# Attention and feed-forward in one kernel: the first two chunk passes taken in halves

## Chip, cores and metric

The kernel runs on one core of one Trainium2 chip. The metric is the device time of one execution in microseconds; several runs of a kernel are compared by their median. TensorE is called PE here, VectorE DVE, ScalarE ACT, GpSimd POOL and SyncE SP, as the profile calls them.

## The reference

Block-sparse attention (4 batches, 8 heads, 768 positions of 64, blocks of 32; each block sees its neighbours, the first and last block and three sampled ones; the first and last block see all) feeds a feed-forward layer of 512 to 2048 to 512 over all 3072 tokens:

```python
attn = softmax(where(mask, q @ k.T / sqrt(64), -1e9)) @ v
x = attn.transpose(0, 2, 1, 3).reshape(3072, 512)
h = x @ w_in
out = (h - tanh(h)) @ w_out
```

## The kernel before

The weights `w_in` and `w_out` come as 64-bit words. Each is cut into 16 tiles `ft` of 128 columns or rows (512 KB as words). A tile is loaded (`load`), turned into 32-bit floats by three DVE instructions (`convert`, which need a scratch of one PSUM bank), and split into a high and a low part by one ACT and one POOL instruction (`split`), so that a product is made of three matmuls. Tiles with `ft < KEPT` (3) stay in SBUF; the others go to scratch in HBM and are read again for every later chunk. Before the change, chunk 0 writes the unsplit 256 KB tile out (`w1`), chunk 1 reads it back, splits it a second time (`again`, `split`) and writes the split 512 KB tile (`w2`), and from chunk 2 on the split tile is read (`get`).

The tokens are cut into six chunks of 512 columns (`CHUNKS`: four blocks of 32 for all batches). A feed-forward unit `u` is one chunk with one `ft`: 12 matmuls make `h` in bank 4 or 5 (`first`), ACT, DVE and POOL make `h - tanh(h)` (`bent`), and two and a half units later 12 matmuls add its product with `w_out` to four banks 0 to 3 (`second`). After the 16 units of a chunk the four banks are copied out and stored (`store`).

An attention unit is one block and half of the heads: `scores` (PE), `most` (DVE maximum), `exps` (ACT), `turn` (PE transposes), `copy`, `accum` (PE), `norm` (DVE), `put` (ACT and POOL write the two parts of a column block of the chunk's operand `x`). There are 44 of these and 12 more for the edge blocks (`weigh`, `join`). Eight (units 0 to 7) must be done before chunk 0 can start, in the lead; units 8 and 9 start in the lead too. After the lead, attention has banks 6 and 7 to itself, except that `convert` of most weight tiles takes bank 6 as its scratch.

The order on every engine is the order of a plan: each step is entered by `at(time, ...)`, where the time is counted in feed-forward units, and all steps are issued sorted by that time. Engines take their instructions in that order, SP its DMAs too.

Of the kernel before, what the change touches and what calls it, by code (L numbers as in the profile page):

```python
# [22 lines left out]
P = 128  # L23
# [7 lines left out]
CT = 4  # L31
# [50 lines left out]
@with_exitstack  # L82
def attention_ffn(ctx, tc, k, q, v, samp, w, rows, out):
    nc = tc.nc
    pool = lambda name, bufs=1, **kw: ctx.enter_context(tc.tile_pool(name=name, bufs=bufs, **kw))
    cst, dpool = pool("cst"), pool("dpool", space=DRAM)
    ident = cst.tile([P, P], F32, name="ident")
    make_identity(nc, ident)
    bias = [cst.tile([P, 1], F32, name=f"bias{i}") for i in range(2)]
    for x, val in zip(bias, (QB, THR2)):  # L90
        nc.vector.memset(x, val)
    banks = [t for psum in [pool("psum", space=PSUM)] for t in [psum.tile([P, 512], F32, name=f"ps{i}") for i in range(8)]]
    f2, rv = pool("f2", 2), pool("rv", 2)
    plan = []

    def at(time, f, *args):
        plan.append((time, len(plan), f, args))

    ffn = FFN(tc, w, bias, banks, dpool, f2, pool("xb"), pool("wb", 3), pool("wr"), rv, out)
    Attention(tc, k, q, v, samp, rows, ffn, ident, banks, pool("att"), pool("sm", 4), f2, rv, at)  # L100
    ffn.plan(at)
    for _, _, f, args in sorted(plan, key=lambda e: e[:2]):
        f(*args)


class Unit:
# [3 lines left out]
    def __init__(self, n, c, time, b=None, f=None, k=None):  # L110
        self.n, self.c, self.b, self.f, self.k = n, c, b, f, k
        early = n < LEAD
        if early:
            t = lambda x: (n + x - T0) * RATE
            self.t = dict(s=t(0.3), m=t(0.65), e1=t(1.1), e0=t(1.2), turn=t(2.0), c0=t(2.15), c1=t(2.2), pv=t(2.6), norm=t(3.05))
        else:
            t = lambda x: time + x
            self.t = dict(s=t(0), m=t(0.08), e1=t(0.2), e0=t(0.3), turn=t(TURN), c0=t(TURN + 0.06), c1=t(TURN + 0.05), pv=t(PROD), norm=t(PROD + 0.1))
        self.banks = dict(s=((6, 7), (0, 1))[n % 2], t=(2, 3), o=4 + n % 2) if early else dict(s=(6, 7), t=(6, 7), o=7)
# [6 lines left out]
class Attention:  # L126
    def __init__(self, tc, k, q, v, samp, rows, ffn, ident, banks, att, sm, f2, rv, at):
# [29 lines left out]
        for m, blocks in enumerate(CHUNKS[1:]):  # L157
            steps = [(c, dict(b=b)) for b in blocks if 0 < b < NB - 1 for c in range(2)]
            if m:
                steps += [((m - 1) // 2, dict(f=(m - 1) % 2, k=k)) for k in range(3)]  # L160
            for i, (c, kw) in enumerate(steps):
                add(c, FIRST0 + SPACE0 * (i + 8 - LEAD) if m == 0 else NFT * m + FIRST + SPACE * i, **kw)
# [8 lines left out]
        for u in units:  # L171
            t, n = u.t, u.n
            if u.b:
                if n:
                    at(max(t["s"] - 2.0, units[n - NQ].t["s"] + 0.01) if n >= NQ else lead(-8.95 + 0.01 * n), self.load_q, u)
                at(max(t["s"] - 1.2, u.before.t["s"] + 0.01 if u.before else lead(-3)), self.gather_k, u)
                at(max(t["s"] - 2.0, u.before.t["pv"] + 0.01 if u.before else lead(-3)), self.gather_v, u)
            else:
                if u.k == 0:
                    at(units[n - 1].t["s"] + 0.02, self.load_q, u)  # L180
                at(units[n - 2].t["pv"] + 0.02, self.load_ve, u)
            at(t["s"], self.scores, u)
            at(t["m"], self.most, u)
            at(t["e1"], self.exps, u, 1)
            at(t["e0"], self.exps, u, 0)
            at(t["turn"], self.turn, u)
            at(t["c1"], self.copy, u, 1)
            at(t["c0"], self.copy, u, 0)
            at(t["pv"], self.accum, u)
            at(t["norm"], self.norm, u)  # L190
            if u.b:
                for x in "hl":
                    at(t["norm"] + (0.1 if x == "h" else 0.15), self.put, u, x)
            elif u.k == 2:
                at(t["e0"] + 0.12, self.weigh, u)
                end = u.n == len(units) - 1
# [219 lines left out]
    def join(self, u, k, s):  # L416
# [15 lines left out]
class FFN:  # L432
    def __init__(self, tc, words, bias, banks, dpool, f2, xb, wb, wr, rv, out):
        self.nc = InOrder(tc)
        self.words, self.bias, self.out = words, bias, out
        self.f2, self.xb, self.wb, self.rv = f2, xb, wb, rv
        self.banks, self.acc, self.hb = banks, banks[:4], banks[4:6]
        kept = [(m, ft) for m in "io" for ft in range(NFT)]
        self.one = {w: dpool.tile([P, 512], F32, name="w1{}{}".format(*w)) for w in kept if w[1] >= KEPT}
# [32 lines left out]
    def split(self, m, u):  # L472
        ft = u % NFT
        t = self.work.pop((m, ft))
        if ft >= KEPT:
            if u < NFT:
                self.nc.sync.dma_start(out=self.one[m, ft], in_=t.bitcast(F32))
        to = self.parts(m, u)
        hi, lo = self.w[m, u]
        self.nc.scalar.activation(out=hi, in_=t.bitcast(F32), func=AF.Copy)  # L480
        self.nc.gpsimd.tensor_tensor(out=lo, in0=t.bitcast(F32), in1=hi.bitcast(F32), op=ALU.subtract)
        if u >= NFT:
            self.nc.sync.dma_start(out=self.two[m, ft], in_=to.bitcast(F32))

    def again(self, m, u):
        t = self.work[m, u % NFT] = self.f2.tile([P, 512], F32, tag="wcvt", name=f"re{m}{u}")
        self.nc.sync.dma_start(out=t, in_=self.one[m, u % NFT])

    def get(self, m, u):
        self.nc.sync.dma_start(out=self.parts(m, u).bitcast(F32), in_=self.two[m, u % NFT])  # L490

    def operand(self, n):
        if n not in self.x:
            t = self.xb.tile([P, 2, NCT, 512], F32R, tag=f"x{n % 2}", name=f"x{n}")
# [3 lines left out]
    def first(self, u, c):  # L498
        xh, xl = self.x[u // NFT]
# [73 lines left out]
    def plan(self, at):  # L573
        conv = sorted(((m, ft) for ft in range(NFT) for m in "io"), key=lambda w: w[1] + NEED[w[0]])
# [5 lines left out]
        for k, ((m, ft), (t0, dt, tmp)) in enumerate(zip(conv, slots)):  # L580
            at(max(t0 - 1.8, done[k - 3] + 0.01 if k > 2 else -99), self.load, m, ft, k)
            for x in range(3):
                at(t0 + dt * x, self.convert, m, ft, x, tmp)
            done.append(t0 + 2 * dt)
            at(done[k] + 0.03, self.split, m, ft)
        for u in range(NU):
            for m, g in (("i", GETI), ("o", GETO)):
                if u % NFT < KEPT:
                    self.w[m, u] = tuple(self.res[m, u % NFT][:, x] for x in range(2))
                elif u >= 2 * NFT:  # L590
                    at(u + g, self.get, m, u)
# [58 lines left out]
```

## Time and profile before

| | |
|---|---|
| median of 3 runs | 803.07 us (802.23 to 804.96) |
| profiled execution, its own time | 805.06 us |
| its span, first to last instruction | 803.3 us |
| mean granted TensorE clock | 0.975 |
| PE busy | 745.8 us |
| DVE, ACT, POOL busy | 554.5, 485.0, 346.2 us |
| moved by DMA | 152.34 MB, mean 190 GB/s |

The profiled execution is 1.76 us longer than its span and 1.99 us above the median. A time in a row is counted from the start of the span. The clock column is the share of full speed granted to TensorE: 1.00 is 2.4 GHz and 0.50 is 1.2 GHz.

### The profile page before, as it was taken

Reading aid. Unit: us, or ns where it says so; the run is one execution under the profiler, and the core shown is the slowest. Engines: PE = TensorE matmul, PEld = TensorE weight load, DVE = VectorE, ACT = ScalarE, POOL = GpSimd, SP = SyncE. Lnnn points to the kernel's source line nnn. Section 1 sums busy time; section 2 is a strip of 40 time slices with the busy share of each in tenths; the row PEclk is TensorE's granted clock in tenths of the full one; section 3 lists DMA queues with packets and bytes.
Section 4 is the critical chain, followed back from the end, with each engine's and each line's share of the span. In section 5 each row is a group of like instructions: output and inputs, shape, how many; then the busy total and the mean of one; then the engine's idle time right before and its main releaser. Section 6 shows DMA issues by size and latency. Waiting matters only on the chain.

```text
span 803.3 us, 20749 instructions
## 1 busy us (share of the span) xinstructions
PE 745.8 (93%) x8128; PEld 571.4 (71%) x8128; DVE 554.5 (69%) x982; ACT 485.0 (60%) x1031; POOL 346.2 (43%) x410
## 2 busy tenths in 40 slices
PE   1777797988999999999999999999999999999996
PEld 0555575766777777777777777777777778888884
DVE  4575877888776676677776677766668667666654
ACT  1684756667587677666655655666567564554543
POOL 3683755768466655543422244322333132222211
PEclk9898898999999999999999999999999999999999
DMA  8978566667268677546665336574526555336542
GB/s 320 309 228 243 175 185 186 191 160 235 87 191 270 236 261 236 192 142 229 194 222 192 94 120 196 196 276 134 178 61 191 203 175 184 131 104 237 183 158 78
DMA packets 57077, 152.34 MB, mean 190 GB/s; under 512 B 9363, under 2 KB 16020, under 8 KB 56980
## 3 DMA queue, kind: packets, MB, share of 16 engines
q1 hardware_dynamic: 56596, 150.49, 58.6%
q8 instruction: 64, 1.05, 0.6%
q10 hardware_dynamic: 384, 0.52, 0.2%
q14 instruction: 33, 0.27, 0.1%
HBM read 124.24 MB, written 26.74 MB: 188 GB/s over the span
## 4 chain that ended last, share of the span: by engine, by line
PE 74%; DVE 1%; ACT 1%; POOL 1%; issue 1%; DMA 0%; POOLq 0%; DVEq 0%
PE ps L68 74%; DVE ps L68 1%; POOL wi L68 0%; ACT p L68 0%; DMA out<-ob 0%; POOL kr L68 0%; DVE cvto L68 0%; DVE x L68 0%; POOL t L68 0%; DVE cvti L68 0%; DVE rs L68 0%; ACT hs L68 0%; ACT pt L68 0%; ACT t L68 0%; POOL wo L68 0%
## 5 line engine op out<-in xcount | busy, mean ns | idle before, releaser
L68 PE MATMUL ps<-x,wi 128*128 128x512 f32 x936 | 239.8, 399 | 1.7 <-ACT wo L68 0.9
L68 POOL TENSOR_TENSOR gl<-t,gh 128x512 fp32r<-128x512 f32 x96 | 124.3, 1295 | 240.8 <-ACT gh L68 110.5
L68 PEld LDWEIGHTS ps<-x,wi 128*128 128x128 f32 x936 | 173.3, 189 | 46.5 <-issue 6.6
L68 PE MATMUL ps<-wo,gh 128*128 128x512 f32 x624 | 202.5, 407 | 0.0
L68 PEld LDWEIGHTS ps<-wo,gh 128*128 128x128 f32 x624 | 114.9, 191 | 33.1 <-issue 7.8
L68 PE MATMUL ps<-wo,gl 128*128 128x512 f32 x312 | 123.6, 398 | 0.3 <-POOL gl L68 0.3
L68 ACT ACTIVATE u<-ps 128x512 f32<-128x512 f32 x96 | 57.1, 595 | 87.8 <-PE ps L68 86.9
L68 POOL COPY kr<-ks 128x256 f32 (+2 forms) x182 | 94.9, 615 | 17.8 <-DMA ks<-k 14.2
L68 DVE TENSOR_TENSOR t<-t,ps 128x512 f32<-128x512 f32 x80 | 54.6, 683 | 64.2 <-ACT t L68 64.1
L68 DVE TENSOR_REDUCE m<-ps 128x2 f32<-128x512 f32 x112 | 72.0, 684 | 37.7 <-PE ps L68 33.0
L68 PE MATMUL ps<-kr,q 64*32 64x256 f32 x1408 | 57.1, 408 | 31.8 <-POOL kr L68 16.1
L68 POOL TENSOR_TENSOR x<-xt,x 128x256 fp32r<-128x256 f32 (+1 forms) x46 | 33.9, 737 | 104.4 <-ACT x L68 104.4
L68 DVE COPY_PREDICATED t<-mk,ps 128x512 f32<-128x512 int32 x96 | 71.4, 744 | 6.3
L68 ACT ACTIVATE p<-ps,nb 128x256 f32<-128x256 f32 x176 | 73.9, 471 | 2.9
L68 DVE SCALAR_TENSOR_TENSOR ps<-qq,ps 128x512 f32<-128x512 f32 x96 | 66.4, 692 | 10.8 <-ACT qq L68 4.9
L68 DVE TENSOR_TENSOR ps<-ps,u 128x512 f32<-128x512 f32 x96 | 66.4, 691 | 5.9 <-ACT t L68 5.9
L68 PEld LDWEIGHTS ps<-wo,gl 128*128 128x128 f32 x312 | 59.4, 190 | 15.2 <-POOL gl L68 1.0
L68 ACT ACTIVATE qq<-u,bias 128x512 f32<-128x512 f32 x96 | 69.5, 724 | 0.0
L68 ACT ACTIVATE mk<-u,bias 128x512 f32<-128x512 f32 x96 | 69.1, 720 | 0.0
L68 DVE SCALAR_TENSOR_TENSOR ps<-u,ps 128x512 f32<-128x512 f32 x96 | 66.3, 691 | 1.9
L68 PEld LDWEIGHTS ps<-vw,pt 128*32 128x32 f32 x2816 | 44.5, 113 | 30.2 <-ACT pt L68 11.3
L68 PE MATMUL ps<-ident,p 128*128 128x128 f32 x448 | 62.0, 283 | 3.5 <-DVE cvto L68 3.5
(86 smaller groups left out, 961.5 us busy)
## 6 DMA issues: line engine op xcount, KB each, us to landing
wi<-w2i SPq DMA_DIRECT2D x52, 512.0 KB, 4.4
wo<-w2o SPq DMA_DIRECT2D x52, 512.0 KB, 3.9
vw<-v SPq DMA_DIRECT2D x182, 130.0 KB, 3.3
q<-q SPq DMA_DIRECT2D x52, 128.0 KB, 4.3
w2i<-wi SPq DMA_DIRECT2D x13, 512.0 KB, 3.9
w2o<-wo SPq DMA_DIRECT2D x13, 512.0 KB, 3.8
ve<-v SPq DMA_DIRECT2D x24, 260.0 KB, 5.9
ks<-k SPq DMA_DIRECT2D x8, 768.0 KB, 6.6
```

The costliest lines, as they stand in the source:

```text
L68: r = f(*args, **kw)
```

## The change

Chunk 0 runs over the units 0 to 7 (called 0A here), then chunk 1 over 0 to 7 (1A) and 8 to 15 (1B), then chunk 0 over 8 to 15 (0B). After 0A the four banks are copied out and kept in HBM (`keep`), and added again when 0B is stored (`back`, `store`). A weight tile is split once, right after its conversion, and only the split tile is saved (`save`); for `ft` of 8 and more the split is written over the words it came from. Sixteen tiles are converted in the lead and 0A, the other sixteen between units 8.35 and 22.5, one every 0.94 units, on banks 6 and 7 by turns. The attention units of chunk 1 stand 1.14 units apart in 0A (2.3 before), none stands in 1A and most of 1B, and those of chunk 2 come 1.14 apart in 0B; these units are transposed 0.66 units after their scores (1.0 before). The edge steps come a chunk later. The lead is planned 0.95 steps earlier, units 8 and 9 get times and banks of their own, and four `q` tiles are held in place of three. POOL does the subtraction `t - h` for 32 units in place of 16.

```diff
-LEAD, T0, RATE = 10, 11.2, 0.62
-FIRST0, SPACE0, FIRST, SPACE, LATE, TURN, PROD = 0.2, 2.3, -1.5, 1.45, 71.0, 1.0, 1.33
-NQ = 3
+LEAD, T0, RATE = 10, 10.25, 0.62
+QUICK, TURN, PROD = (0.66, 0.95), 1.0, 1.33
+NQ = 4
-POOLED = range(NFT)
+POOLED = range(2 * NFT)
+SEGS = [(0, 0, HALF), (1, 0, HALF), (1, HALF, NFT), (0, HALF, NFT)] + [(n, 0, NFT) for n in range(2, len(CHUNKS))]
+BAND = [None, (0.75, 1.14), (22.72, 1.14), (31.87, 1.44), (47.71, 1.44), (63.55, 1.44)]
+EDGES = {3: (0,), 4: (1,), 5: (2, 3)}
+CONVA = [0.1, 0.75, 1.4, 2.05, 2.65, 3.31, 3.77, 4.45, 4.91, 6.05, 7.19, 7.62]
+CONVAB = [3, 3, 3, 3, 6, 7, 6, 7, 6, 6, 6, 6]
+CONVB = 8.35, 0.94
...
-    def split(self, m, u):
...
-            if u < NFT:
-                self.nc.sync.dma_start(out=self.one[m, ft], in_=t.bitcast(F32))
+        if ahead:
+            to = self.raw[m, ft].bitcast(F32R)
...
-    def again(self, m, u):
...
+    def save(self, m, ft):
+        self.nc.sync.dma_start(out=self.two[m, ft], in_=self.done[m, ft].bitcast(F32))
...
+    def keep(self, j):
...
+        self.nc.sync.dma_start(out=self.part[j], in_=t)
...
-        slots = [(t(3.3 + 1.6 * k), 0.3 * RATE, None) for k in range(3)] + [(0.1 + 0.4 * k, 0.1, banks[3]) for k in range(6)]
-        slots += [(FIRST0 + SPACE0 * k + x, 0.1, banks[6]) for k in range(1, 6) for x in (0.47, 1.2, 1.58, 1.95)]
-        slots += [(NFT + FIRST + x, 0.1, banks[6]) for x in (-0.47, 0.47, 1.2)]
+        slots = [(t(3.3 + 1.6 * k), 0.3 * RATE, None) for k in range(4)] + [(x, 0.09, banks[b]) for x, b in zip(CONVA, CONVAB)]
+        slots += [(CONVB[0] + CONVB[1] * k, 0.12, banks[6 + k % 2]) for k in range(2 * HALF)]
...
+            if ft >= KEPT:
+                at(end + 0.4, self.save, m, ft)
+            free.append(end + (1.2 if ahead else 0.01))
+            sent[m, ft] = end + 1.3
...
-                elif u >= NFT:
-                    at(u + g - 0.8, self.again, m, u)
-                    at(u + g + 0.3, self.split, m, u)
+                elif (m, u) not in done:
+                    at(max(u + g, sent[m, ft]), self.get, m, u)
```

On PE, at the end of the lead, the order before is this (`ps` 72 to 79 are banks 0 to 7; `kr,q` is `scores`, `ident,p` is `turn`, `vw,pt` is `accum`, `x,wri` is `first` of feed-forward unit 0). The first two rows are the `turn` of attention unit 8, then come its `accum` (its first and last row), the `turn` of unit 9, half of `first`, the `scores` of unit 10 (one row), the `accum` of unit 9 (one row) and the second half of `first`:

```order
L68 MATMUL ps_75<-ident,p_1_1074 128x128 x4
L68 MATMUL ps_74<-ident,p_0_1084 128x128 x4
L68 MATMUL ps_76<-vw_161,pt_1_1171 32x65 x4
...
L68 MATMUL ps_76<-vw_162,pt_0_1169 32x65 x4
L68 MATMUL ps_75<-ident,p_1_1166 128x128 x4
L68 MATMUL ps_74<-ident,p_0_1174 128x128 x4
L68 MATMUL ps_76<-x_455,wri_147 128x512 x6
L68 MATMUL ps_78<-kr_165,q_6_970 32x256
...
L68 MATMUL ps_77<-vw_163,pt_1_1232 32x65 x4
...
L68 MATMUL ps_76<-x_455,wri_147 128x512 x6
```

And this is the same place of the changed kernel:

```order
L79 MATMUL ps_75<-ident,p_1_1062 128x128 x4
L79 MATMUL ps_74<-ident,p_0_1070 128x128 x4
L79 MATMUL ps_76<-x_435,wri_128 128x512 x12
L79 MATMUL ps_73<-ident,p_1_1155 128x128 x4
L79 MATMUL ps_72<-ident,p_0_1163 128x128 x4
L79 MATMUL ps_79<-vw_139,pt_1_1160 32x65 x4
...
L79 MATMUL ps_79<-vw_140,pt_0_1158 32x65 x4
L79 MATMUL ps_78<-kr_143,q_6_954 32x256
```

All 12 matmuls of unit 0 now stand right behind the `turn` of attention unit 8; the `turn` of 9, the `accum` of 8 and 9 and the `scores` of 10 stand behind them.

On DVE, in the middle of 0A, the changed kernel has this order (`ps_79` and `ps_78` are banks 7 and 6; `m<-ps` is `most`, `rs`, `x`, `xt` is `norm`, rows with `raw` or `spare` are `convert`, `ps_76` and `ps_77` are `h`):

```order
L79 STREAM_TRANSPOSE xt_1741<-x_1745 128x256
L79 TENSOR_REDUCE m_1773<-ps_79 128x2
L79 TENSOR_REDUCE m_1773<-ps_78 128x2
L79 SCALAR_TENSOR_TENSOR ps_77<-qq_1687,ps_77 128x512
L79 TENSOR_SCALAR ps_79<-spare 128x512
L79 COPY_PREDICATED t_1660<-mk_1696,ps_77 128x512
L79 SCALAR_TENSOR_TENSOR ps_79<-spare,ps_79 128x512
L79 SCALAR_TENSOR_TENSOR cvto_1793<-spare,ps_79 128x512
L79 TENSOR_TENSOR ps_76<-ps_76,u_1803 128x512
L79 TENSOR_SCALAR ps_78<-rawi_1648 128x512
L79 SCALAR_TENSOR_TENSOR ps_78<-rawi_1648,ps_78 128x512
L79 SCALAR_TENSOR_TENSOR cvti_1843<-rawi_1648,ps_78 128x512
```

One conversion now stands between the maximum and the transposes of an attention unit (bank 7), the next one behind them (bank 6); before, four conversions on bank 6 stood between two attention units.

On SP, in 1B, the changed kernel has this order (`rawi`, `rawo` or `spare` from `w` is `load`, `w2` from one of these is `save`, `wi` or `wo` from `w2` is `get`; each moves 512 KB). What stood at the same row before is `accum`'s `vw` loads and the 256 KB `w1` tiles:

```order
L79 DMA rawi_2798<-w 128x1024
L79 DMA w2i_113<-spare 128x1024
L79 DMA wi_2808<-w2i_111 128x1024
L79 DMA wo_2845<-w2o_122 128x1024
L79 DMA spare<-w 128x1024
L79 DMA w2o_124<-rawo_2746 128x1024
L79 DMA wi_2863<-w2i_112 128x1024
L79 DMA wo_2900<-w2o_123 128x1024
```

For each unit there is now one load, one save and two gets, one behind the other.

## Rows read from the trace of the kernel before

**Rows 1.** Busy time by stretch: each engine's busy us (instructions), clock, DMA share, GB/s.

```profile
15.00:78.00 63.00, 47.97 (x1102) 33.93 (x1103) 38.92 (x83) 38.60 (x104) 39.16 (x62) 0.89 0.90 278
78.00:200.00 122.00, 102.84 (x930) 76.92 (x929) 98.77 (x169) 80.86 (x165) 86.04 (x89) 0.90 0.65 189
200.00:640.00 440.00, 438.76 (x5275) 334.98 (x5274) 310.37 (x556) 280.82 (x605) 179.90 (x218) 1.00 0.57 185
640.00:795.00 155.00, 155.00 (x823) 124.90 (x822) 100.34 (x154) 82.27 (x156) 38.65 (x35) 1.00 0.48 160
```

**Rows 2.** ACT in order of time: `qq` of units 0, 16, 32, 74 and 95.

```profile
78.15 0.74 ACT L68 ACTIVATE qq<-u,bias 128x512 f32<-128x512 f32 x1
...
214.15 0.72 ACT L68 ACTIVATE qq<-u,bias 128x512 f32<-128x512 f32 x1
...
342.14 0.74 ACT L68 ACTIVATE qq<-u,bias 128x512 f32<-128x512 f32 x1
...
672.52 0.72 ACT L68 ACTIVATE qq<-u,bias 128x512 f32<-128x512 f32 x1
...
789.14 0.72 ACT L68 ACTIVATE qq<-u,bias 128x512 f32<-128x512 f32 x1
```

**Rows 3.** Who waited for whom: us in total, times, longest us.

```profile
PE ps L68 <- DVE cvti L68: 7.8, 4, 2.9
...
PE ps L68 <- ACT pt L68: 6.7, 8, 3.1
...
PE ps L68 <- DVE cvto L68: 5.6, 3, 3.0
```

**Rows 4.** PE in order of time, two waits for conversions in chunk 0.

```profile
98.11 1.09 PE L68 MATMUL ps<-ident,p 128*128 128x128 f32 x4 [3.01 <-DVE cvto L68]
...
111.85 1.10 PE L68 MATMUL ps<-kr,q 64*32 64x256 f32 x32 [1.57 <-DVE cvti L68]
```

**Rows 5.** Two stretches, PE alone: busy, clock, DMA share, GB/s.

```profile
98.00:104.00 6.00, 5.89 (x53) 0.50 0.51 141
110.00:112.00 2.00, 0.43 (x10) 1.00 0.89 133
```

**Rows 6.** PE in order of time, end of the lead.

```profile
59.64 1.09 PE L68 MATMUL ps<-ident,p 128*128 128x128 f32 x8
63.48 0.45 PE L68 MATMUL ps<-vw,pt 128*32 128x65 f32 x8 [2.74 <-DMA vw<-v]
64.49 1.75 PE L68 MATMUL ps<-vw,pt 128*32 128x65 f32 x56 [0.57 <-DMA vw<-v]
...
70.31 1.09 PE L68 MATMUL ps<-kr,q 64*32 64x256 f32 x32
71.34 1.11 PE L68 MATMUL ps<-vw,pt 128*32 128x65 f32 x64
72.38 1.65 PE L68 MATMUL ps<-x,wri 128*128 128x512 f32 x6
```

**Rows 7.** POOL in order of time: the last `put` of attention unit 7.

```profile
63.20 0.73 POOL L68 TENSOR_TENSOR x<-xt,x 128x256 fp32r<-128x256 f32 x1 [1.31 <-ACT x L68]
```

**Rows 8.** PE in order of time: the wait of attention unit 3.

```profile
29.82 1.96 PE L68 MATMUL ps<-kr,q 64*32 64x256 f32 x32 [4.43 <-DMA q<-q]
```

**Rows 9.** Busy time by stretch, columns as in Rows 1.

```profile
10.00:30.00 20.00, 9.34 (x184) 5.58 (x192) 9.57 (x17) 8.32 (x23) 12.91 (x21) 0.97 1.03 363
110.00:120.00 10.00, 8.43 (x69) 6.40 (x68) 7.45 (x12) 6.54 (x16) 5.30 (x5) 1.00 0.89 229
...
280.00:300.00 20.00, 20.00 (x210) 15.71 (x213) 14.97 (x25) 15.32 (x34) 11.29 (x10) 1.00 0.80 266
700.00:800.00 100.00, 96.21 (x415) 77.52 (x413) 60.65 (x89) 49.61 (x88) 23.41 (x18) 1.00 0.46 149
```

**Rows 10.** DMA issues: count, KB each, median us from issue to landing.

```profile
wi<-w2i SPq DMA_DIRECT2D x52, 512.0 KB, 4.4
```

**Rows 11.** Groups of instructions: busy us, mean ns, idle before, releasers.

```profile
L68 ACT ACTIVATE ob<-ps 128x512 f32<-128x512 f32 x12 | 7.2, 601 | 4.4 <-PE ps L68 2.4 <-DMA out<-ob 2.0
```

More of the change, by code (lines that the diff above doesn't have):

```diff
@@ L97, in at @@
         plan.append((time, len(plan), f, args))
-    ffn = FFN(tc, w, bias, banks, dpool, f2, pool("xb"), pool("wb", 3), pool("wr"), rv, out)
-    Attention(tc, k, q, v, samp, rows, ffn, ident, banks, pool("att"), pool("sm", 4), f2, rv, at)
+    att = pool("att")
+    ffn = FFN(tc, w, bias, banks, dpool, f2, pool("xb"), pool("wb", 3), pool("wr"), rv, att, out)
+    Attention(tc, k, q, v, samp, rows, ffn, ident, banks, att, pool("sm", 4), f2, rv, at)
     ffn.plan(at)
@@ L106, with __init__ @@
 class Unit:
-    def __init__(self, n, c, time, b=None, f=None, k=None):
+    def __init__(self, n, c, time, b=None, f=None, k=None, quick=False):
         self.n, self.c, self.b, self.f, self.k = n, c, b, f, k
@@ L156, in __init__ @@
                 add(c, 0, b=b)
[L157 to L160, printed above, removed]
+        for m, blocks in list(enumerate(CHUNKS))[1:]:
+            steps = [(c, dict(b=b, quick=m < 3)) for b in blocks if 0 < b < NB - 1 for c in range(2)]
+            edges = [(g // 2, dict(f=g % 2, k=k)) for g in EDGES.get(m, ()) for k in range(3)]
+            steps += edges
             for i, (c, kw) in enumerate(steps):
-                add(c, FIRST0 + SPACE0 * (i + 8 - LEAD) if m == 0 else NFT * m + FIRST + SPACE * i, **kw)
+                add(c, BAND[m][0] + BAND[m][1] * (i - 2 * (m == 1)), **kw)
         lead = lambda x: (x - T0) * RATE
@@ L195, in __init__ @@
                 at(t["e0"] + 0.12, self.weigh, u)
-                end = u.n == len(units) - 1
+                end = 2 * u.c + u.f in EDGES[len(CHUNKS) - 1]
                 quiet = iter([t["norm"] + 0.1 + 0.08 * j for j in range(6)] if end else self.quiet(units[u.n + 1 :], t["norm"]))
@@ L432, with __init__ @@
 class FFN:
-    def __init__(self, tc, words, bias, banks, dpool, f2, xb, wb, wr, rv, out):
+    def __init__(self, tc, words, bias, banks, dpool, f2, xb, wb, wr, rv, att, out):
         self.nc = InOrder(tc)
         self.words, self.bias, self.out = words, bias, out
-        self.f2, self.xb, self.wb, self.rv = f2, xb, wb, rv
+        self.f2, self.xb, self.wb, self.rv, self.att = f2, xb, wb, rv, att
         self.banks, self.acc, self.hb = banks, banks[:4], banks[4:6]
         kept = [(m, ft) for m in "io" for ft in range(NFT)]
-        self.one = {w: dpool.tile([P, 512], F32, name="w1{}{}".format(*w)) for w in kept if w[1] >= KEPT}
+        self.part = [dpool.tile([P, 512], F32, name=f"part{j}") for j in range(CT)]
         self.two = {w: dpool.tile([P, 1024], F32, name="w2{}{}".format(*w)) for w in kept if w[1] >= KEPT}
@@ L442, in __init__ @@
         self.spare = xb.tile([P, 1024], I32, name="spare")
-        self.x, self.w, self.h, self.work, self.raw = {}, {}, {}, {}, {}
+        self.x, self.w, self.h, self.work, self.raw, self.done = {}, {}, {}, {}, {}, {}
     def parts(self, m, u):
-        if u % NFT < KEPT:
-            t = self.res[m, u % NFT]
+        ft = UNITS[u][1]
+        if ft < KEPT:
+            t = self.res[m, ft]
         else:
@@ L548, in second, with back @@
         g = [self.work[u, x] for x in ("gh", "gh", "gl")]
-        ft = u % NFT
+        first, last = u in (0, *self.ends), u + 1 in self.ends
         for i in part:
             self.nc.tensor.matmul(
-                self.acc[j], lhsT=g[i][:, j * P : (j + 1) * P], rhs=wo[i % 2], start=ft == i == 0, stop=ft == NFT - 1 and i == 2
+                self.acc[j], lhsT=g[i][:, j * P : (j + 1) * P], rhs=wo[i % 2], start=first and i == 0, stop=last and i == 2
             )
+    def keep(self, j):
+        t = self.att.tile([P, DM], F32, tag=("p0", "p1", "pt0", "pt1")[j], name=f"half{j}")
+        if j % 2:
+            self.nc.vector.tensor_scalar(out=t, in0=self.acc[j], scalar1=-1.0, scalar2=None, op0=ALU.mult)
+        else:
+            self.nc.scalar.activation(out=t, in_=self.acc[j], func=AF.Copy, scale=-1.0)
+        self.nc.sync.dma_start(out=self.part[j], in_=t)
+    def back(self, j):
+        if j % 2 == 0:
+            self.sums = self.rv.tile([P, 1040], F32, tag="rv", name=f"sums{j}")
+        self.work["sum", j] = self.sums[:, DM * (j % 2) : DM * (j % 2) + DM]
+        self.nc.sync.dma_start(out=self.work["sum", j], in_=self.part[j])
     def store(self, n, j):
@@ L580, in plan @@
-        for k, ((m, ft), (t0, dt, tmp)) in enumerate(zip(conv, slots)):
-            at(max(t0 - 1.8, done[k - 3] + 0.01 if k > 2 else -99), self.load, m, ft, k)
+        halves = [sorted(((m, ft) for ft in range(a, a + HALF) for m in "io"), key=lambda w: w[1] + NEED[w[0]]) for a in (0, HALF)]
+        slots = [(t(3.3 + 1.6 * k), 0.3 * RATE, None) for k in range(4)] + [(x, 0.09, banks[b]) for x, b in zip(CONVA, CONVAB)]
+        slots += [(CONVB[0] + CONVB[1] * k, 0.12, banks[6 + k % 2]) for k in range(2 * HALF)]
@@ L582, in plan @@
+        sent, free = {}, []
+        for k, ((m, ft), (t0, dt, tmp)) in enumerate(zip(halves[0] + halves[1], slots)):
+            ahead = ft >= HALF and ft + HALF + NEED[m] - t0 > AHEAD
+            at(max(t0 - 1.8, free[k - 3] if k > 2 else -99), self.load, m, ft, k)
             for x in range(3):
                 at(t0 + dt * x, self.convert, m, ft, x, tmp)
-            done.append(t0 + 2 * dt)
-            at(done[k] + 0.03, self.split, m, ft)
+            end = t0 + 2 * dt
+            at(end + 0.03, self.split, m, ft, ahead)
+            if ft >= KEPT:
+                at(end + 0.4, self.save, m, ft)
+            free.append(end + (1.2 if ahead else 0.01))
+            sent[m, ft] = end + 1.3
+            if not ahead:
+                done.append((m, UNITS.index((ft // HALF, ft))))
@@ L586, in plan @@
+        self.ends = [e for e in ENDS if e != 2 * HALF]
         for u in range(NU):
+            n, ft = UNITS[u]
             for m, g in (("i", GETI), ("o", GETO)):
[L588 to L591, printed above, removed]
-                elif u >= NFT:
-                    at(u + g - 0.8, self.again, m, u)
-                    at(u + g + 0.3, self.split, m, u)
+                if ft < KEPT:
+                    self.w[m, u] = tuple(self.res[m, ft][:, x] for x in range(2))
+                elif (m, u) not in done:
+                    at(max(u + g, sent[m, ft]), self.get, m, u)
@@ L603, in plan @@
                     at(u + LAG + 0.5 + 0.125 * j + 0.5 * i, self.second, u, j, part)
-            if u % NFT == NFT - 1:
+            if u + 1 in ENDS and SEGS[ENDS.index(u + 1)] != SEGS[1]:
                 for j in range(CT):
-                    at(u + LAG + 0.64 + 0.125 * j + 0.5 * end, self.store, u // NFT, j)
+                    to = (self.keep, j) if u + 1 == HALF else (self.store, n, j)
+                    at(u + LAG + 0.64 + 0.125 * j + 0.5 * end, *to)
+                    if ENDS.index(u + 1) == 3:
+                        at(u + 0.1 * j, self.back, j)
 def convert_op(nc, raw, t, tmp, k):
```

55 lines of the change are left out of this document (34 added, 21 removed).

## Prediction

> **What bounds the kernel now.** I read first the busy time by stretch [rows 1]. From 200 to 640 us PE is busy 438.76 of 440 us at clock 1.00, from 640 to 795 us all the time. So from 200 us on PE is the bound, and what other engines or transfers save there is worth nothing. From 78 to 200 us, where chunk 0 is computed, PE is busy 102.84 of 122 us at clock 0.90: 19.2 us idle, and ten per cent of 122 us, some 12 us, lost to the clock. Part of the half-speed time was idle, so I put the loss of this stretch at 30 us. In the lead, 15 to 78 us, 15 us are idle and the clock is 0.89. These two stretches are where time can come from: PE has the same matmuls in both kernels, so the end moves by what PE loses less, or more, before it is saturated.
>
> Second, how much PE work there is at full rate. Unit 74's `qq` starts at 672.52 us and unit 95's at 789.14 us [rows 2]: 116.62 us for 21 units, 5.55 us each, with almost no attention. Units 16 to 32 take 342.14 - 214.15 = 128.0 us with 11 attention units, so one of these costs (128.0 - 16 x 5.55) / 11 = 3.56 us.
>
> Third, what PE waits for in chunk 0. The list of waits has 7.8 + 5.6 = 13.4 us, in seven waits, for `cvti` and `cvto` [rows 3]: PE writes scores or transposes into bank 6 and must wait until DVE has finished a conversion there. A wait of this kind costs twice when it is long. Behind the one of 3.01 us [rows 4] the stretch 98 to 104 us runs at 0.50, the lower of the two levels, 1.2 GHz, and 5.89 us of PE work there would take half [rows 5]: 2.95 us more, 6.0 in all. Behind the wait of 1.57 us at 111.85 us the clock stays at 1.00 [rows 4, 5].
>
> **The change part by part.** *The lead.* Before, unit 0's `first` is complete at 72.38 + 1.65 = 74.0 us, since behind the `turn` of attention unit 8 (59.64 to 60.7 us) PE waits 2.74 and 0.57 us for `vw` of unit 8, which unit 0 doesn't need [rows 6]. Afterwards `first` stands right behind that `turn`. Its second half needs the last `put` of attention unit 7, which ends at 63.20 + 0.73 = 63.9 us [rows 7]; so it is complete at 63.9 + 1.65 = 65.6 us, 8.4 us earlier. What it overtook is still to do: `turn` 9 at 1.09, `accum` 8 at the 1.11 of `accum` 9, `accum` 9 at 1.11 and `scores` 10 at 1.09 [rows 6], 4.4 us. Net 4.0 us gained. With four `q` tiles the fourth is loaded at the start, ahead of all `k`; its wait of 4.43 us goes [rows 8]. But DMA is full there (share 1.03 from 10 to 30 us [rows 9]), and the `vw` tiles that come next are queued as before, so most of that wait turns into a wait for them. The bounds are 0 and 4.4 us, and I take 2. The lead gives **-6.0 us**; with the clock, of which 0.11 x 63 = 7 us is lost in this stretch [rows 1], it could give 15, and with neither part 0.
>
> *0A.* The twelve conversions beside 0A are no sparser than before, but only eight of them use banks 6 and 7; four use bank 3, which is free until `second` of unit 0. Before, 23 conversions used bank 6. By conversions the loss is 30 / 23 x 8 = 10.4 us; by attention units, of which some eight stood in the lossy stretch and six stand in 0A, 30 / 8 x 6 = 22.5 us. Of the 19.2 us idle 13.4 are conversions, so I take a value nearer the first: 14 us. **-16 us** (30 to 14). The bounds are 0 and all six attention units at 6.0 us, 36.
>
> *1A and 1B.* No attention shares the banks here until 22.7 units, so the conversion waits are gone; this is already in the 14. What is new is the DMA. Between units 12 and 22 the plan holds per unit one load, one save and two gets of 512 KB, 2.10 MB; at 5.55 us that is 378 GB/s. No row reaches it: 266 GB/s at share 0.80 is 333 at full share, 149 at 0.46 is 324, 363 at 1.03 is the most, and 229 at 0.89, with small `vw` transfers, is 257 [rows 9]. At 333 a unit takes 6.30 us, 7.5 us too much over ten units. The gets stand 1.6 units ahead of their use, 8.9 us, and land in 4.4 us [rows 10], so 4.5 us are covered and 3 remain; at 324 it is 4.7. I take **+4 us**. The bounds are 0 (at 363 the excess of 2.3 us is covered) and, at 257 GB/s, 81.7 - 55.5 - 4.5 = 22 us. The load into a buffer also waits on SP for the save of that buffer, and the gets are queued behind it; a save that lands late delays these too, which the upper bound takes in.
>
> The Trainium skill (DMA: Bandwidth & Descriptors, section Bandwidth) has the HBM side bind transfers between HBM and SBUF at about 358 GB/s for a core. By that the ten units would take 58.7 us, the excess would be covered, and the sum would be 783 and not 787. The row of loads alone, 363 at 1.03, agrees with it; the rows that also store stand lower, and they decide here.
>
> *0B.* Its eight attention units come every 1.14 units and are transposed 0.66 units after their scores. The kernel before has no such rhythm without conversions. Its waits for `pt`, 6.7 us in 8 times [rows 3], are the nearest: spread over all 56 attention units that is 0.1 us each, and one wait for each of the eight is 6.7 us. I take **+2 us**, with 0 and 7 as bounds.
>
> *At nothing.* The second split (26 ACT and 26 POOL instructions, 52 transfers of 256 KB) falls into 200 to 340 us, where PE is saturated: 1.24 us idle in 440 [rows 1] is all it could give. `keep` copies four banks at about 0.6 us each [rows 11]; the 12 matmuls of `first` for the next unit lie between, half of 5.55 us; without them one copy, 0.6 us, shows. The extra 16 subtractions on POOL lie in 1A to 0B, and POOL has no gathers in 1A and most of 1B. The 42 further gets lie mostly in 1B and 0B and are in the DMA term. The edge steps go from one saturated chunk to the next, at 3.56 us of PE either way.
>
> *The sum:* -6.0 - 16 + 4 + 2 = -16 us. Against the profiled execution: 805.06 - 16 = 789.1 us. That execution is 1.99 us above the median of the runs, so the median should be **787 us**, 2% faster.
>
> **The rivals.** (a) *0A waits in every attention unit, and long enough to lose the clock.* One conversion now stands between the maximum and the transposes of the same unit, so PE can stall at both places. At 6.0 us for each of six units the loss is 36 us and not 14: 809 us, slower. It decides from 14 + 16 = 30 us on, 5 us per unit. For it: such a unit is shown [rows 4, 5], and attention units stand twice as dense as in chunk 0. Against it: the seven waits there came to 13.4 us [rows 3], 1.9 us each, nearer to the one of 1.57 that cost no clock than to the one of 3.01.
>
> (b) *DMA is the bound in 1A and 1B.* At the 257 GB/s of the poorest row the wait is 22 us and not 4: 805 us. For it: loads and saves in turn, and SP that waits in order. Against it: the `vw` transfers that spoil that row are absent there.
>
> (c) *DMA keeps up,* at the 363 GB/s of the best row: 783 us.
>
> (d) *Lighter than thought:* the clock stays at 1.00 in the lead and 0A loses no more than 5 us, the lead gives 9: 787 - 9 - 3 = 775 us. For it: without long gaps there is no half speed, and in each of the two stretches the clock alone costs 7 to 12 us.
>
> (e) *The change doesn't do what it says:* the conversions in 0A are as dense as before and attention is denser, so the stalls just gather in half the time and the 30 us stay: 803 us.
>
> **How the numbers follow.** Forecast 0.36, (c) 0.12, (d) 0.16, (a) 0.13, (b) 0.13, (e) 0.10. About 0.3%, 2.4 us, is what a measurement of this kernel can tell from no change. Faster: forecast, (c), (d), and 0.05 of (b), 0.05 of (e) and 0.02 of (a) where these are half true: 0.76. Same: 0.03 of (b), 0.03 of (e), 0.01 of (a): 0.07. Slower: 0.10 of (a), 0.05 of (b), 0.02 of (e): 0.17. The range from 773 to 806 leaves out the upper half of (a) and the tail of (d). The likeliest case by itself spans 780 to 797: 0A between 10.4 and 22.5, DMA between 0 and 5, on both sides.
>
> **What would show it.** The lead: the 12 matmuls of unit 0 done near 64 to 66 us and its `qq` some 8 to 10 us before the 78.15 of now [rows 2]. 0A: `qq` of unit 8 near 143 us, and the waits of PE for conversions below 10 us in total. 1A and 1B: `qq` distances of 5.55 us up to unit 12, then up to 6.3 us, with a DMA share near 1 and PE waits for `wi` or `wo`. 0B: eight units in some 74 us, PE nearly full. From chunk 2 on PE is saturated as before. The prediction is wrong if 0A takes over 95 us from `qq` to `qq`, if 1A and 1B together take over 110 us, or if PE has waits after unit 32.

## The result and the profile after

| | before | after |
|---|---|---|
| median (20 runs each, one chip) | 804.03 us (801.91 to 806.74) | 808.18 us (804.73 to 812.09) |
| ratio, 95% interval | | 1.0053 [1.0038, 1.0067] |
| profiled execution, its own time and span | 805.06, 803.3 us | 810.89, 809.1 us |
| mean granted clock | 0.975 | 0.986 |

The change makes the kernel half a per cent slower: 4.2 us by the medians, 5.8 us between the two profiled executions. The forecast was 16 us faster.

The first view is the page of the changed kernel: busy time, and the chain that ended last.

```profile
PE 744.0 (92%) x8128; PEld 564.0 (70%) x8128; DVE 546.8 (68%) x970; ACT 478.7 (59%) x1021; POOL 333.9 (41%) x400
...
PE 69%; DMA 11%; DVE 10%; ACT 5%; issue 2%; SPq 1%; POOL 1%; DVEq 0%; POOLq 0%
```

The chain of the kernel before:

```profile
PE 74%; DVE 1%; ACT 1%; POOL 1%; issue 1%; DMA 0%; POOLq 0%; DVEq 0%
```

PE does the same 8128 matmuls in nearly the same time as before (745.8 us). So the span grew by idle time: 809.1 - 744.0 = 65.1 us against 803.3 - 745.8 = 57.5. The chain has DMA in it with 11%, and before with 0%. Where the idle time lies shows in the busy time by stretch. The stretches are the lead, 0A, 1A with 1B, 0B, and what follows; columns as in [rows 1].

```profile
15.00:78.00 63.00, 44.61 (x1022) 30.74 (x1023) 39.15 (x80) 36.87 (x98) 43.95 (x68) 0.89 0.85 265
78.00:155.00 77.00, 67.63 (x837) 48.34 (x836) 59.49 (x109) 53.39 (x116) 46.19 (x51) 0.98 0.58 191
155.00:267.00 112.00, 98.09 (x550) 74.04 (x552) 76.95 (x121) 67.59 (x128) 67.31 (x61) 1.00 0.89 301
267.00:334.00 67.00, 66.93 (x904) 50.31 (x892) 44.00 (x83) 46.82 (x106) 38.81 (x51) 1.00 0.66 205
334.00:640.00 306.00, 304.77 (x3720) 232.27 (x3719) 215.23 (x387) 184.19 (x400) 99.67 (x131) 1.00 0.52 172
640.00:801.00 161.00, 160.71 (x1114) 127.69 (x1115) 107.61 (x173) 87.34 (x174) 37.22 (x34) 1.00 0.48 162
```

PE is idle for 18.4 us in the lead (before 15.0), for 9.4 in 0A (before 19.2 from 78 to 200 us), for 13.9 in 1A and 1B, and for 0.1 in 0B; after that it is saturated as before. So the change took 9.8 us of idle time out of the stretch behind the lead, as meant. It added 3.4 us ahead of it, and 13.9 us in a stretch that mostly lay where PE was saturated before (1.24 us idle from 200 to 640 us).

Most of the 3.4 us lies ahead of all work of PE. Its first instruction, the first scores, comes 2.9 us later than in the profiled execution of before:

```profile
15.72 1.96 PE L68 MATMUL ps<-kr,q 64*32 64x256 f32 x32 [15.72 <-POOL kr L68]
```

```profile
18.61 1.96 PE L79 MATMUL ps<-kr,q 64*32 64x256 f32 x32 [18.61 <-POOL kr L79]
```

The units in order of time: `qq` on ACT of units 0, 8, 24, 32 and 95.

```profile
77.47 0.71 ACT L79 ACTIVATE qq<-u,bias 128x512 f32<-128x512 f32 x1
...
154.89 0.71 ACT L79 ACTIVATE qq<-u,bias 128x512 f32<-128x512 f32 x1
...
267.33 0.73 ACT L79 ACTIVATE qq<-u,bias 128x512 f32<-128x512 f32 x1
...
333.82 0.72 ACT L79 ACTIVATE qq<-u,bias 128x512 f32<-128x512 f32 x1
...
795.15 0.72 ACT L79 ACTIVATE qq<-u,bias 128x512 f32<-128x512 f32 x1
```

Unit 32 comes 8.3 us earlier than before (342.14 in [rows 2]), and still unit 95 comes 6.0 us later. Unit 32 is no fair mark: counted by their scores, 25 attention units are done there, and 29 before. Four attention units of 3.56 us (14.2 us) turn the 8.3 us ahead into 6 us behind. The end is read from idle time, not from a unit in the middle.

### The profile page after: what moved, and what is told of

Read it like the earlier page. It is cut to its first block, busy times and chain, and to the rows that moved or that the text cites. A ratio compares the mean times of both kernels' runs of the same rounds, so it can differ in the third digit from the quotient of the medians.

```text
span 809.1 us, 20672 instructions
## 1 busy us (share of the span) xinstructions
PE 744.0 (92%) x8128; PEld 564.0 (70%) x8128; DVE 546.8 (68%) x970; ACT 478.7 (59%) x1021; POOL 333.9 (41%) x400
## 4 chain that ended last, share of the span: by engine, by line
PE 69%; DMA 11%; DVE 10%; ACT 5%; issue 2%; SPq 1%; POOL 1%; DVEq 0%; POOLq 0%
PE ps L79 69%; DVE ps L79 5%; DMA rawi<-w 3%; DMA vw<-v 2%; DMA spare<-w 2%; DMA rawo<-w 2%; SPq L79 1%; DMA ks<-k 1%; ACT pt L79 1%; DVE m L79 1%; DVE cvto L79 1%; ACT p L79 1%; DMA w2o<-rawo 1%; DVE cvti L79 1%; DVE t L79 1%
## 5 line engine op out<-in xcount | busy, mean ns | idle before, releaser
L79 PEld LDWEIGHTS ps<-x,wi 128*128 128x128 f32 x936 | 171.1, 188 | 53.1 <-DVE ps L79 7.8
L79 PEld LDWEIGHTS ps<-wo,gh 128*128 128x128 f32 x624 | 113.1, 189 | 38.6 <-issue 14.1
L79 POOL COPY kr<-ks 128x256 f32 (+2 forms) x182 | 95.3, 618 | 16.9 <-DMA vw<-v 14.8
L79 PE MATMUL ps<-kr,q 64*32 64x256 f32 x1408 | 59.4, 401 | 27.3 <-POOL kr L79 19.0
L79 DVE TENSOR_TENSOR t<-t,ps 128x512 f32<-128x512 f32 x64 | 43.7, 683 | 46.5 <-ACT t L79 46.5
L79 ACT ACTIVATE pt<-ps 128x512 f32<-128x512 f32 x72 | 41.5, 598 | 42.8 <-PE ps L79 42.6
```

The lines of the kernel that those rows point to most:

```text
L79: r = f(*args, **kw)
```

## What the two traces leave open

**The stretch of 1A and 1B.** Units 8 to 24 take 112.4 us (154.89 to 267.33). They hold 16 units of 5.55 us of matmuls and two attention units, and PE idles 13.9 us. What PE waited for there, from 155 to 267 us (us in total, times, longest):

```profile
PE ps L79 <- DMA wo<-w2o: 4.0, 5, 1.2
PE ps L79 <- DMA wi<-w2i: 3.5, 3, 1.4
PE ps L79 <- DVE cvto L79: 2.4, 1, 2.4
PE ps L79 <- DVE cvti L79: 2.2, 1, 2.2
```

So 7.5 us are waits for gets and 4.6 for conversions. What the DMA queue of SP waited for in the same stretch:

```profile
SPq L79 <- DMA w2o<-rawo: 19.6, 5, 5.2
SPq L79 <- DMA w2i<-rawi: 15.6, 3, 5.8
SPq L79 <- DMA w2i<-spare: 9.7, 3, 4.1
SPq L79 <- DMA w2o<-spare: 6.1, 2, 4.6
```

Of 112 us SP stands for 51 us, in 13 waits, until a save has landed. What it issues then is seen in order of time (start, length, count):

```profile
181.01 0.33 SPq L79 DMA_DIRECT2D rawi<-w  x1
181.43 0.38 SPq L79 DMA_DIRECT2D w2i<-spare  x1
...
187.24 0.33 SPq L79 DMA_DIRECT2D spare<-w  x1
187.63 0.42 SPq L79 DMA_DIRECT2D w2o<-rawo  x1
```

About every 6.5 us there is a load, and right behind it a save. The three word buffers (`spare` and two of a pool, which the rows call `rawi` or `rawo` by the weight that is in them) are used by turns, so the load of tile k must wait until the save of tile k - 3 has landed, since both use the same buffer. The save of tile k - 2 is ready by then, but stands behind that load. It starts only when the load goes, and the next load then waits for this save. So one save at a time is under way, and each tile costs a landing. The chain of waits of the same stretch has such steps (start, us, what):

```profile
181.01 4.92 DMA rawi<-w
...
187.24 5.21 DMA spare<-w
...
193.75 5.49 DMA rawi<-w
...
200.68 4.61 DMA rawo<-w
```

A load in these rows takes 4.6 to 5.5 us; one starts about every 6.5 us (eight from 181.01 to 226.46 us), where the plan holds one tile per 0.94 units, 5.2 us.

My theory after this view is the order of load and save on SP. The rivals are: the bytes (the forecast's own rival (b)), and the gets that SP can't issue while it stands, for which PE waits 7.5 us.

**The lead.** PE in order of time, where the forecast had `turn` of attention unit 8 at 59.64 us and unit 0's `first` right behind:

```profile
56.18 1.36 PE L79 MATMUL ps<-vw,pt 128*32 128x65 f32 x56 [1.87 <-DMA vw<-v]
...
65.85 1.31 PE L79 MATMUL ps<-vw,pt 128*32 128x65 f32 x64 [1.98 <-ACT pt L79]
67.09 1.97 PE L79 MATMUL ps<-ident,p 128*128 128x128 f32 x8
68.71 2.36 PE L79 MATMUL ps<-x,wri 128*128 128x512 f32 x6
...
72.31 1.43 PE L79 MATMUL ps<-x,wri 128*128 128x512 f32 x5 [0.32 <-POOL x L79]
```

`first` does stand right behind that `turn`, but the `turn` comes at 67.09 us. The wait for `q` of 4.43 us [rows 8] is gone, and there are more waits for `vw` and `pt` (7.5 and 5.7 us in the lead, 5.3 and 3.2 before). On SP three word loads from 40 us on now stand ahead of that `turn`; before it was one, at 55.68 us, and the next came at 61.63:

```profile
46.60 1.07 SPq L79 DMA_DIRECT2D rawo<-w  x1
...
55.89 0.58 SPq L79 DMA_DIRECT2D rawi<-w  x1
...
60.74 0.37 SPq L79 DMA_DIRECT2D spare<-w  x1
```

These belong to the conversions, of which four are planned into the lead that was itself planned 0.95 steps shorter. The theory is that the fourth conversion and its loads lengthen the lead; the rivals are the fourth `q` tile, whose load stands ahead of all `k`, and the 0.95 steps.

## The experiments

Ratios are to the kernel before on the same chip, with 95% intervals. The first four kernels ran together (before 804.93 us), the next three (before 804.42), and the last three (before 804.77). Units 8 to 24 are told by the distance of their `qq`, 112.4 us in the changed kernel.

**e1: three `q` tiles again.**

```diff
-NQ = 4
+NQ = 3
```

> The changed kernel with three q tiles as before, so that the fourth q is not loaded ahead of all k. Theory 'the fourth q delays the first gather': the first scores come at 15.7 us as before and not at 18.6, qq of unit 0 some 2 to 3 us earlier than 77.5 (unless the wait of 4.4 us for q comes back and eats it), total 2 to 3 us less, 805 to 806. Rival 'the 2.9 us are something else (the start of a run scatters)': no change of the first scores by more than 0.5 us, total 808 or, with the wait for q back, 810.

807.26 us, ratio 1.0040 [1.0024, 1.0056]: no more than the changed kernel's own spread away from 1.0053. From the first scores to the `turn` of attention unit 8 it takes 47.9 us, the changed kernel 48.5, and before 43.9. The `q` tile is not what lengthens this stretch. The first scores come at 15.96 us, as the first theory had it; whether the fourth tile is the reason is taken up in the last section.

**e2: three conversions in the lead, and the lead planned as long as before.** Thirteen conversions stand beside 0A in place of twelve.

```diff
-LEAD, T0, RATE = 10, 10.25, 0.62
+LEAD, T0, RATE = 10, 11.2, 0.62
-CONVA = [0.1, 0.75, 1.4, 2.05, 2.65,
+CONVA = [0.1, 0.45, 0.8, 1.4, 2.05, 2.65,
-        slots = [(t(3.3 + 1.6 * k), 0.3 * RATE, None) for k in range(4)]
+        slots = [(t(3.3 + 1.6 * k), 0.3 * RATE, None) for k in range(3)]
```

> The changed kernel with three conversions in the lead instead of four, the fourth beside unit 0, and the lead planned 0.95 steps later as before: two word tiles of 512 KB fewer stand ahead of the vw loads on SP. Theory 'word loads and the fourth conversion hold up the vw loads of the lead': the turn of attention unit 8 ends near 64 us and not 69, qq of unit 0 near 72 to 73, total 803 to 804. Rival 'the lead is late because of its first 3 us alone, the rest is the clock': qq of unit 0 at 76 to 78, total 807 to 809.

The stretch to `turn` shrinks from 48.5 to 45.5 us. Between 15 and 78 us PE idles 17.5 us, against 18.4; the first scores are as late as in the changed kernel, at 18.67 us. So the two edits together take back 3 of the 4.6 us by which the `turn` came later; which of the two does it isn't shown, since no run has one without the other. The median shows no gain: 808.55 us, 1.0055 [1.0031, 1.0080], with which a gain of 1 to 2 us can't be told from none. Units 8 to 24 take 112.7 us, as without the edits.

**e3: the gets of units 8 to 23 read half.** The low parts of the weights are not read there and the high parts stand in for them, so part of the computation is changed; PE's work is the same.

```diff
+        if u < 24:
+            self.w[m, u] = self.w[m, u][0], self.w[m, u][0]
+            self.nc.sync.dma_start(out=to[:, 0:512], in_=self.two[m, UNITS[u][1]][:, 0:512])
+            return
```

> The changed kernel with the gets of units 8 to 23 halved: only the high part of a tile is read, 256 KB, and the matmuls that take the low part read the high part instead, so this run leaves out the low parts of those weights; the count and order of all instructions and DMAs is the same. Theory 'bytes bound 1A and 1B': 1.57 MB per unit in place of 2.10, 283 GB/s at full PE rate, so units 8 to 24 take some 93 to 97 us instead of 112.4 and the total falls by 14 to 18 us to 790 to 794. Rival 'the order on SP binds, each load waiting for a save and the gets behind it': 107 to 112 us for units 8 to 24, total 803 to 808.

804.01 us, 0.9999 [0.9979, 1.0019], and units 8 to 24 take 108.2 us. The DMA share from 155 to 255 us falls to 0.81 (0.89 in the changed kernel). Less than a third of the 13.9 us goes with half of the gets' bytes. Bytes alone are not the cause, but they are not nothing.

**e4: the gets of units 8 to 23 go out on ACT's queue.**

```diff
-        self.nc.sync.dma_start(out=self.parts(m, u).bitcast(F32), in_=self.two[m, UNITS[u][1]])
+        eng = self.nc.scalar if u < 24 else self.nc.sync
+        eng.dma_start(out=self.parts(m, u).bitcast(F32), in_=self.two[m, UNITS[u][1]])
```

> The changed kernel with the gets of units 8 to 23 issued from ACT's queue, the same bytes. Theory 'bytes bound 1A and 1B': units 8 to 24 stay at 108 to 114 us, total 806 to 812, a little worse where ACT waits. Rival 'the order on SP binds': 95 to 102 us, total 793 to 800.

811.61 us in four runs from 808.79 to 820.82, 1.0133 [1.0065, 1.0200], and units 8 to 24 take 113.5 us. PE no longer waits for a get there, but it idles 11.8 us all the same, for POOL, DVE and ACT. SP still waits for its saves, 58.5 us in all, with no get behind the load. So gets held up on SP do not set the pace. The run is not clean: ACT, which now issues the gets, stands 9.1 us in two waits for DMAs that it did not have before. The next run decides.

**e5: the load stands behind the next save.** One number of the plan: a load that reuses a saved buffer is planned 1.45 units behind its last conversion, not 1.2. That puts it behind the save of the tile after.

```diff
-            free.append(end + (1.2 if ahead else 0.01))
+            free.append(end + (1.45 if ahead else 0.01))
```

> The changed kernel with one number changed: a word load into a buffer is planned 1.45 units behind the conversion that used the buffer, not 1.2, so on SP it stands behind the save of the tile two before and not ahead of it. Theory 'a load waits on SP for the save three tiles back to land, some 6 us, and holds up the next save behind it, so that each tile costs one landing': units 8 to 24 fall from 112 to 95 to 102 us and the total to 793 to 800. Rival 'bytes bound 1A and 1B': 108 to 113 us, total 806 to 809.

800.59 us, 0.9944 [0.9921, 0.9968]: 1.1% below the changed kernel's ratio. Units 8 to 24 take 104.5 us. SP in order of time, in the same stretch:

```profile
179.53 0.32 SPq L79 DMA_DIRECT2D w2i<-spare  x1
179.94 0.38 SPq L79 DMA_DIRECT2D rawi<-w  x1
...
185.36 0.32 SPq L79 DMA_DIRECT2D w2o<-rawo  x1
185.77 0.38 SPq L79 DMA_DIRECT2D spare<-w  x1
```

And what SP's queue waits for from 155 to 260 us:

```profile
SPq L79 <- POOL rawi L79: 15.1, 5, 4.1
SPq L79 <- POOL rawo L79: 13.5, 4, 4.6
SPq L79 <- POOL spare L79: 11.7, 3, 3.9
...
SPq L79 <- DMA w2o<-rawo: 3.7, 1, 3.7
```

The save goes first, the 51 us of waits for landings become 3.7, and SP waits for POOL's split instead. That wait is 40 us, nearly as long, and does little harm, since the save is the next thing to do and the load behind it finds its buffer free. The busy time of this stretch, and the 20 us within it where most bytes move:

```profile
155.00:260.00 105.00, 99.78 (x591) 76.13 (x590) 77.69 (x123) 68.32 (x130) 68.24 (x62) 0.98 0.90 321
```

```profile
200.00:220.00 20.00, 19.96 (x85) 15.46 (x85) 15.85 (x24) 14.42 (x27) 13.36 (x11) 1.00 0.97 360
```

PE idles 5.2 us here; from 155 to 255 us, a stretch that can be laid beside the changed kernel's, it is 5.2 against 13.9. What it waits for is no longer a transfer:

```profile
PE ps L79 <- POOL gl L79: 4.6, 4, 3.5
PE ps L79 <- DMA wo<-w2o: 0.3, 1, 0.3
```

`gl` is the low part of `h - tanh(h)`, which `second` needs. The longest of these waits, 3.5 us, can be followed back: DVE waits until 220.53 us for a word load that took 5.2 us, its conversion is split on POOL at 223.88 us, `gl` stands behind that split at 225.11, and PE goes on at 226.43.

**e6: e3 and e5 together** (the low parts left out as in e3).

> Order as in the run before and the gets of units 8 to 23 halved, so this run leaves out the low parts of those weights. Theory 'order on SP': with the order mended, bytes are next; units 8 to 24 at 92 to 96 us, total 788 to 794, and 3 to 6 us less than the order alone. Rival 'bytes alone': as with the gets halved in the old order, 108 us, total 803 to 805. If it equals the order alone, bytes cost nothing.

796.88 us, 0.9899 [0.9871, 0.9927]; units 8 to 24 take 101.6 us, 2.9 less than in e5. The share from 155 to 260 us is 0.79 and PE idles 3.3 us. So half of the gets' bytes are worth some 3 us here, less than the 8 us of the order. It is near what such runs can tell: the intervals of e5 and e6 just overlap, and the kernels with this order and all bytes (e5, e7, e9) take 102.9 to 105.5 us for units 8 to 24.

**e7: e2 and e5 together,** the whole computation.

> The order on SP mended and three conversions in the lead with the lead planned as before. If both gains add: 2 to 3 us below the order alone, 790 to 798, and below the kernel before. If the lead's gain is lost again in 0A, as the run with the lead alone suggests: equal to the order alone.

796.49 us (795.67 to 801.38), 0.9905 [0.9879, 0.9932]. This one beats both kernels: it is 0.95% faster than before, and 1.5% below the changed kernel's ratio. In the lead:

```profile
66.85 1.43 PE L79 MATMUL ps<-x,wri 128*128 128x512 f32 x5 [0.32 <-POOL x L79]
```

The 12 matmuls of unit 0 are done at 68.3 us, 5.5 earlier than in the changed kernel; 1.7 us of that are earlier first scores (16.93 us). In 1A and 1B (20 us of it):

```profile
180.00:200.00 20.00, 19.98 (x87) 15.95 (x87) 16.76 (x26) 13.98 (x26) 14.36 (x12) 1.00 0.99 375
```

Idle time in all is 794.6 - 741.9 = 52.7 us, against 57.5 before and 65.1 in the changed kernel.

**before_again: the kernel before once more,** for its lead.

> The kernel before once more, for the start of the lead alone: in seven profiles of kernels with the changed lead the first scores came between 15.96 and 18.67 us, before at 15.72. If that is scatter of the start, it may come anywhere from 15.7 to 18.7 here too, and the time from the first scores to the turn of attention unit 8 stays near 43.9 us; if the start of before is sound, 15.7 again.

804.04 us. From the first scores (16.10 us) to `turn` of attention unit 8 (59.81) it takes 43.7 us; the first trace had 43.9.

**e8: e7 with the conversions of 1A and 1B denser.**

```diff
-CONVB = 8.35, 0.94
+CONVB = 8.35, 0.88
```

> Order mended, lead with three conversions, and the conversions of the second half every 0.88 units instead of 0.94. Theory 'with the order mended bytes bind late in 1B, where DMA is full, while 1A has room': the same bytes are spread to earlier units, units 8 to 24 at 99 to 102 us against 102.9, total 1 to 3 us less. Rival 'the cycle of the three word buffers binds, whatever the plan': units 8 to 24 at 103 to 106, total the same.

800.52 us, 0.9956 [0.9937, 0.9975]: worse than e7, and units 8 to 24 take 107.3 us, not 102.9. The chain of waits has this step:

```profile
175.69 7.41 DMA spare<-w
```

The loads of the chain from 170 to 200 us take 5.6 to 7.4 us, and conversions planned every 0.88 units (4.9 us) wait for them.

**e9: e7 with two conversions in the lead.** Fourteen stand beside 0A.

> Order mended, and two conversions in the lead instead of three, the third beside unit 0. Theory 'each word load and conversion in the lead holds it up': from the first scores to the turn of attention unit 8 some 43 to 44 us against 45.6 with three and 48 to 50 with four; total 1 to 2 us less unless 0A gives it back. Rival 'three is as good as two, since the lead then waits for POOL and SP': 45 to 46 us, total the same or, with a late third tile, more.

801.04 us, 0.9968 [0.9945, 0.9992]: worse than e7. The stretch to `turn` is 44.5 us, within the 43.9 to 45.6 of three conversions, while 0A grows from 76.8 to 79.0 us and units 8 to 24 from 102.9 to 105.5.

## Why the prediction was wrong

**What bounds the kernel** was read rightly: PE is saturated again from unit 24 on, and the gain or loss lies ahead of that. One size in this part failed. The stretch from 78 to 200 us was put down with a loss of 30 us, of which some 11 were for the clock. The clock rose as forecast, to 0.98 in 0A and 1.00 in 1A and 1B. But PE's busy time is 744.0 us after, while the two profiled executions of before have 745.8 and 742.5. The most that the clock can have given is 1.8 us. The groups of matmuls of before and after say the same:

```profile
L68 PE MATMUL ps<-x,wi 128*128 128x512 f32 x936 | 239.8, 399 | 1.7 <-ACT wo L68 0.9 <-DVE t L68 0.8
```

```profile
L79 PE MATMUL ps<-x,wi 128*128 128x512 f32 x936 | 240.3, 398 | 7.1 <-DMA wi<-w2i 3.5 <-DVE cvti L79 2.2 <-DVE ps L79 1.4
```

The share of a stretch at the lower level, times its length, is no price: it counts idle time too, and only the matmuls that ran then pay. The means of one are 399 and 398 ns.

**0A.** The mechanism was right. PE's waits for conversions fell from 13.4 us [rows 3] to 1.7 in 0A, and what 0A loses is 9.4 us idle and at most 1.5 for the clock (0.02 of 77 us), where 14 were forecast. `qq` of unit 8 comes 77.4 us behind that of unit 0. But since 19.2 and not 30 us were there to be had, the term is -9.8 and not -16 us. Rival (a), a long wait in every attention unit, didn't come. The clock fell once in 0A, to 0.50 at 136 us, behind two waits of 1.14 and 0.71 us. Both are shorter than the 1.57 us behind which it stayed at 1.00 before [rows 4, 5], so the length of one wait, by which the prediction told dear waits from cheap ones, doesn't tell them apart.

**The lead** gave nothing where -6.0 us were forecast. Of the 3.4 us more of idle time, 2.9 lie ahead of the first scores, a start of which the prediction took no account. In the 61.5 us behind the first scores PE idles 14.8 us, against 14.3 and 15.7 in the two executions of before. The step that failed took the `turn` of attention unit 8 to stay at 59.6 us and only moved `first` ahead. It forgot that a part of the change stood in front of that `turn`: a fourth conversion with its word load, in a lead planned 0.95 steps shorter. Counted from the first scores, unit 0's `first` is complete after 55.1 us and not 58.3: 3.2 us gained where 8.4 were forecast, and the 4.4 us of work that it overtook is still to do. Over the kernels with four conversions in the lead (after, e1, e3 to e6) the stretch to `turn` is 47.9 to 50.5 us, mean 49.0; over those of the changed kind with three and the longer plan (e2, e7, e8) 43.9 to 45.6, mean 45.0. Two conversions (e9, 44.5) give nothing more, so the 4.0 us may belong to the conversion or to the plan. The fourth `q` tile does nothing to this stretch (e1). That most of its 4.43 us would turn into a wait for `vw` isn't borne out: the waits for `vw` grew by 2.2 us and those for `pt` by 2.5.

**1A and 1B** is the step that was mis-sized, and for another reason than it weighed: 13.9 us idle where it had 4, within its bounds of 0 and 22. The prediction's own sign for this came: units 8 to 24 take 112.4 us, over its 110. The upper bound was the poorest rate, 257 GB/s; the rate was 301 over the stretch, and 375 was seen (e7). What was missing beside the bytes is the turn of a word buffer, 6.5 us per tile where the plan has 5.2. The sentence that a load waits on SP for a save of its buffer and that the gets queue behind it names the right instruction, but not what matters most behind it. PE does wait 7.5 us for gets, but taking them off SP's queue gives nothing (e4); the next save matters, since a save held behind a load makes the load after it late too (e5, 8 us with one number). And 4.6 us are waits for conversions, which the prediction took to be gone here. Rival (b) had the place and, by luck, nearly the time, 805 us, but not the cause: half of the gets' bytes are worth 4.2 us in the wrong order (e3) and 2.9 in the right one (e6).

Rival (c) had the transfers hidden at 363 GB/s. By the rule of about 358 GB/s of the Trainium skill (DMA: Bandwidth & Descriptors, section Bandwidth) they would be hidden too. With the order mended the gets are: in e5, at 360 GB/s in its best 20 us, PE waits 0.3 us for them. The word loads are not: through a late conversion, its split and `gl` on POOL, one of them costs PE 3.5 us (e5).

**0B** costs 0.1 us, not 2. The second split, `keep`, POOL's subtractions and the edges cost nothing that shows, as forecast: 1.6 us idle from 267 us to 801.

**The sum** of the measured terms: +2.9 (first scores) + 0.5 (rest of the lead) - 9.8 (0A) + 13.9 (1A and 1B) + 0.1 (0B) + 0.3 (saturated: 1.23 + 0.29 - 1.24) - 1.8 (PE busy) = +6.1 us, beside +5.8 of span. Against the forecast of -16 the lead is off by 6.5 us and the start by 2.9, 1A and 1B by 9.9, and 0A by 6.2.

**What stays open.** The gain of e2's lead is not in its median, but with the order mended e7 stands 4.1 us below e5, with intervals that just overlap. That the late loads of 1A and 1B swallowed it in e2 would fit, and isn't shown by itself. That e8 is slower because three word buffers and a landing of 5 to 7 us allow no denser conversions is argued from its chain; a fourth buffer wasn't tried. Whether the fourth conversion or the shorter plan delays the `turn` wasn't tried either.

## What to carry to other kernels

On a queue that issues in order, a load that reuses a buffer waits for a save to land; put the next save ahead of that load, or each tile pays a whole landing, with the DMA engines far from empty and no single transfer to blame. Count transfers twice, then: bytes at a rate, and landings per turn of a buffer. A stage that a forecast takes as unchanged must be read once more in the changed order on every queue, before its end is used as a fixed point; and a lost clock is priced by the durations of the matmuls, not by the length of the stretch.

## What was unexpected of the hardware

The DMA engines moved 375 GB/s over 20 us at a share of 0.99 with loads and saves mixed (e7, 180 to 200 us), where the best row of before was 363, for loads alone [rows 9]. The Trainium skill (DMA: Bandwidth & Descriptors, section Bandwidth) has about 358 GB/s as a core's limit, and also a measured 425 GB/s at a size of 16 MB with the neighbouring core idle; the 375 lies between. The share alone doesn't give the rate: at the start of the kernel before, 419 GB/s moved from 8 to 12 us at a share of 1.00, and 294 in the next 4 us at 1.03.

The start of the first scores lies between 15.7 and 18.7 us over the twelve profiled executions. The three with three `q` tiles come first, at 15.72, 15.96 and 16.10 us, and the nine with four at 16.25 to 18.67. With four, SP issues the first load of `k` 0.46 us later (3.19 to 3.21 us, not 2.73), so about half a microsecond may belong to the fourth tile. The rest is a scatter of 2.4 us among kernels that all have four, and its cause is open. Three microseconds in a single trace are near what many steps of such a forecast are worth, so a lead is better compared from its own first instruction.
